# Seven block products for the last eight tiles of the odd batches, and where the weight blocks are stored

## Chip, cores and metric

The kernel runs on one core of one Trainium2 chip. The metric is the device time of one execution in microseconds; before the change it is 752.98 us, the median of 3 runs (750.64 to 752.99). The profile is one execution with a span of 752.0 us.

The engines have short names: PE is TensorE (matmuls, with PEld for its weight loads), DVE is VectorE, ACT is ScalarE, POOL is GpSimd, SP is SyncE. SPq is the queue of transfers (DMA) that SP issues, one after the other in the program's order.

## What is computed

```python
# x (8, 8, 512, 64), state (8, 8, 32, 64): batch, head, token, width
a = softmax(scale * x @ state^T);    xread = a @ state
a2 = softmax(scale * state @ x^T);   sread = a2 @ x
t = concat([xread, sread], axis=2)          # 544 rows for each batch
t = t.transpose(0, 2, 1, 3).reshape(4352, 512)
h = t @ w_in                                # w_in (512, 2048)
g = h * cos(h)                              # the gate
out = g @ w_out                             # w_out (2048, 512)
```

All matmuls are in float32. The weights come as 64-bit floats and are converted on the chip in the first part of the run.

## The kernel before

**Tiles and steps.** The program is one list of tiles. A tile is a slice of 128 of the 2048 columns of h, for the 512 tokens of one batch: 16 tiles f for each of 8 batches b, 128 in all; 16 further tiles at the end serve the state rows. Each step of the outer loop (line 1281) works on one tile, and 32 steps (two batches, a *pair*) make a period. A batch's first eight tiles and its last eight are two phases: phases 0 and 1 are the even batch's, 2 and 3 the odd batch's.

**First layer.** The attention matrix aT (256 rows of softmax weights by 512 tokens) is multiplied with the product of state and w_in (`sw`). In batches 0 and 1 and in phase 3 of the later odd batches this is done plainly: `hidden` (line 485) issues two matmuls of 512 columns for each tile. Elsewhere two tiles that are neighbours share a scheme of seven products of blocks with half the size in each direction, in place of the eight that the blocks of a 2 x 2 product need: `seven_part` (line 529) issues seven matmuls of 256 columns in four parts, two parts in the even step and two in the odd one. It wants more from other engines: `sw_sums` (line 518) makes four sums of 128 x 128 on POOL, three steps ahead; ACT copies two half banks after part 0 (lines 544, 545), before part 1 may add to them; DVE makes two sums in PSUM (`seven_sum`, line 547), one behind part 1 and one behind part 2. `seven` (line 501) says which tiles do this.

**Gate.** ACT rounds h (`gate`, line 561), DVE takes the difference (`gate2`, 564), ACT takes the sine (`gate3`, 567), DVE multiplies (`gate4`, 581, the gate product) and writes g to SBUF. `gate4` frees the PSUM bank into which the first layer of a later tile goes.

**Second layer.** The product of g and w_out is done for a pair of batches with seven products at the outer level ("p1" to "p7"), each of which again has seven block products. g is stored in `quads`, groups of four tiles; `quads_free` lists those that are free. The *outer sums* of quads (`outer_sum`, line 1097, at line 706) are differences of whole quads before a product; their steps are in a table (line 1086). Each block product is a stage (`stage`, line 746) with four matmuls of 256 columns (line 759) against a block of weights that was fetched from DRAM into a ring of four buffers (`fetch_block`, line 693). When a stage has been issued, the fetch for the third stage after it is issued too, and waits until its buffer is free.

**Weight blocks.** w_out gives four matrices a11, a12, a21, a22. Seven matrices (these or sums of them) are each kept in DRAM as eight blocks in `blocks_kept`: numbers 0, 1, 7 and 3 are raw quarters of the matrix, 4, 5, 6 and 2 are sums, made by POOL in `inner_weights` (line 664) and stored by `send` (line 676). Five of the seven are made in steps 7 to 26. Two are late: a22 (number 2) is overwritten in step 18, so it is stored whole in `kept` in step 17 (`move`, line 1106), and read back a quarter at a time in steps 41 to 44 by `late_weights` (line 1113), which then makes its sums in step 45 and stores all eight blocks in steps 46 to 51; a12 (number 1) stays in SBUF, and its eight blocks are stored in steps 52 to 56.

**Order.** Nothing is scheduled by a tool: every engine works in the order in which the program issues. In the first period `first_pair` (line 1186) sets it: `go(n)` issues the attention work that is planned for the step, then come `gate3` and `gate4`. After the tile's work the loop issues what `weights_at` and then `outer_at` hold for the step (lines 1305 to 1308), and at the step's end the loads of x (`load_now`). All transfers but a few share SPq, so a store that waits there holds back the fetches behind it.

Of the kernel before, what the change touches and what calls it, by code (L numbers as in the profile page):

```python
# [10 lines left out]
F32 = mybir.dt.float32  # L11
I32 = mybir.dt.int32
U32 = mybir.dt.uint32
ALU = mybir.AluOpType
# [8 lines left out]
def kernel(  # L23
# [8 lines left out]
    nc = tc.nc  # L32

    B, H, S, D = x.shape
    Ns = state.shape[2]
    Dm, Dff = moe_w_in.shape
    P = 128
# [33 lines left out]
    QT, NQUAD = 4, 12  # L71
# [4 lines left out]
    def quad(n):  # L76
        return g_all[:, QT * n:QT * n + QT]

    def matrix(n):
        return quad(n).rearrange("p t (u d) -> p (t u) d", d=HD)  # L80

    a11, a12, a21, a22 = [matrix(n) for n in range(5, 9)]
# [4 lines left out]
            for i in range(NB)]  # L87
    spare = ctx.enter_context(tc.tile_pool(name="spare", bufs=1,
                                           space=bass.MemoryType.DRAM))
    blocks_kept = spare.tile([7, 8, P, QT * P], F32)  # L90
    kept = spare.tile([QT, P, S], F32)

    xT = consts.tile([P, NK, S], F32)
    x_b = consts.tile([P, NC, H, D], F32)
# [404 lines left out]
    LO, HI = slice(0, HS), slice(HS, S)  # L499

    def seven(t):
        return t.pair is not None and t.b > 1 and t.phase < 3

    def halves(b, n):
        aT, aS = aT_of[b], aS_all[:, b % 2]
# [102 lines left out]
    later, stores_due, totals_due, now = [], [], [], [0]  # L608
# [50 lines left out]
    def quarters(m):  # L659

        m = m.rearrange("p (k i) (m d) -> p m k i d", k=2, m=2)
        return m[:, 0, 0], m[:, 0, 1], m[:, 1, 0], m[:, 1, 1]

    def inner_weights(which, m, temps, pieces=range(4), send_at=None):

        m11, m12, m21, m22 = quarters(m)
        t1, t2, t3, t4 = [temps[:, n].rearrange("p (i d) -> p i d", d=P)
                          for n in range(4)]
        for i in pieces:
            o, x1, x2, op = ((t1, m21, m22, ALU.add),  # L670
                             (t2, t1, m11, ALU.subtract),
                             (t3, m11, m21, ALU.subtract),
                             (t4, m12, t2, ALU.subtract))[i]
            nc.gpsimd.tensor_tensor(o, x1, x2, op=op)

        def send(i):
            block = (m11, m12, m22, m21, t1, t2, t3, t4)[i]
            nc.sync.dma_start(
                out=blocks_kept[which, (0, 1, 3, 7, 4, 5, 6, 2)[i]].rearrange(
                    "p (i d) -> p i d", d=P),  # L680
                in_=block)

        if send_at is None:
            for i in range(4 if 3 in pieces else 0):
                send(i)
                stores_due.append(lambda i=i: send(4 + i))
        else:
            for i, step in enumerate(send_at):
                weights_at[step].append(lambda i=i: send(i))
# [363 lines left out]
    for i, t in enumerate(all_tiles):  # L1053
        t.mate = all_tiles[i ^ 1]
    pairs = [all_tiles[2 * NF * n].pair for n in range(B // 2)]
    stage_at, sums_at, outer_at, weights_at = [defaultdict(list)
                                               for _ in range(4)]
    PERIOD, STAGES = 2 * NF, len(ORDER)
    ROWS = {"p1": 0, "p2": 1, "p5": 0, "p3": 3, "p6": 0, "p7": 2, "p4": 1}

# [22 lines left out]
    dve, pool = nc.vector, nc.gpsimd  # L1083
    for n in range(B // 2):
        end = n == B // 2 - 1
        for r, engine, o, x1, x2, half in (
                ((20, 25) if n == 0 else (25, 26), dve, 0, 2, 0, 0),
                ((27 - (not n), 28), dve, 0, 2, 0, 1), ((31, 31), pool, 2, 3, 2, 0), ((33, 33), dve, 0, 3, 0, 0),
                ((34, 34 + (not end)), dve, 0, 3, 0, 1),
                ((35, 36), dve, 2, 3, 2, 1),  # L1090
                ((38 - end,) * 2, pool, 1, 1, 0, 0),
                ((39 - end,) * 2, pool, 1, 1, 0, 1)):
            for i in range(2):
                outer_at[PERIOD * n + r[i]].append(
                    (engine, n, o, x1, x2, half, i))

    def outer_sum(engine, n, o, x1, x2, half, i):
        o, x1, x2 = [quad(quads_of[n, r][half])[:, 2 * i:2 * i + 2]
                     for r in (o, x1, x2)]
        sub(engine, o, x1, x2)  # L1100
# [2 lines left out]
        o_, x1_, x2_ = [quad(q)[:, 2 * i:2 * i + 2] for q in (o, x1, x2)]  # L1103
        nc.vector.tensor_tensor(o_, x1_, x2_, op=op)

    def move(to_dram, q, i):
        sb = quad(q)[:, i]
        o, x = (kept[i], sb) if to_dram else (sb, kept[i])
        nc.sync.dma_start(out=o, in_=x)

    late_quads = []

    def late_weights(step):
        if step == 41:
            late_quads.append(quads_free.pop(0))
        if step < 45:
            move(False, late_quads[0], step - 41)
        if step == 45:
            late_quads.append(quads_free.pop(0))
            inner_weights(2, matrix(late_quads[0]), quad(late_quads[1]),  # L1120
                          send_at=(46, 46, 47, 47, 49, 49, 50, 51))
        elif step == 52:
            quads_free.append(late_quads[0])
            inner_weights(1, a12, quad(late_quads[1]),
                          send_at=(52, 52, 53, 53, 54, 54, 55, 56))
        elif step == 57:
            quads_free.extend([A12, late_quads[1]])

    A11, A12, A21, A22, SQ = 5, 6, 7, 8, 11
    temps = [quad(TEMPS), aS_all.rearrange("p n i s -> p (n i s)").rearrange(  # L1130
        "p (t s) -> p t s", s=S)]
    for i in range(QT):
        weights_at[7 + i].append(lambda i=i: inner_weights(
            0, a11, temps[0], (i,), () if i < 3 else (15,) * 4 + (16,) * 4))
        weights_at[17].append(lambda i=i: move(True, A22, i))
    for steps, o, x1, x2, op in (
            ((18, 19), A21, A11, A21, ALU.subtract),
            ((22, 23), SQ, A12, A22, ALU.subtract)):
        for i in range(2):
            weights_at[steps[i]].append(  # L1140
                lambda o=o, x1=x1, x2=x2, op=op, i=i: weight_sum(
                    o, x1, x2, op, i))
# [4 lines left out]
            nc.gpsimd.tensor_tensor(o_, x1_, x2_, op=op)  # L1147

    for at_, what in (
            (15, lambda: quads_free.append(10)),  # L1150
            (16, lambda: pool_sum(SQ, A21, A22, ALU.add)),
            (17, lambda: quads_free.append(9)),
            (17, lambda: inner_weights(3, matrix(SQ), temps[1])),
            (18, lambda: pool_sum(A22, SQ, A11, ALU.subtract)),
            (20, lambda: inner_weights(5, matrix(A21), temps[0])),
            (22, lambda: inner_weights(4, matrix(A22), temps[1])),
            (23, lambda: quads_free.append(A11)),
            (24, lambda: inner_weights(6, matrix(SQ), temps[0])),
            (25, lambda: quads_free.append(A21)),
            (27, lambda: quads_free.append(A22)),  # L1160
            (27, lambda: quads_free.append(TEMPS)),
            (28, lambda: quads_free.append(SQ))):
        weights_at[at_].append(what)
    for step in (41, 42, 43, 44, 45, 52, 57):
        weights_at[step].append(lambda step=step: late_weights(step))

    n_stages = 0
# [14 lines left out]
    def go(n):  # L1182
        for p in todo[n]:
            part(*p)

    def first_pair(step, t):
        last, conv = conv_at.get(step - 1, -1), conv_at.get(step, -1)
        if step == 4:
            warm(1, acc[0])
        if step != 1:  # L1190
            hidden(t)
        if step == 0:
            hidden(all_tiles[1])
            warm(3, acc[0])
            gate(t)
            gate2(t)
            convert(3, "bcdf")
            convert(4, "1")
            go(0)
        else:  # L1200
            go(0)
            if step == 5:
                states(1, side_banks[0])
            gate(t)
            gate2(t)
            if step == 3:
                warm(4, acc[0])
                part(0, "products", 1, SIDE)
            go(1)
            go(3)  # L1210
            if step == 1:
                convert(4, "bcdf")
            elif last >= 0 and step < 5:
                convert(last, "bcdf")
            if conv >= 0 and not todo[1]:
                convert(conv, "1")
        gate3(t)
        go(5)
        if step == 3:
            part(0, "products_kept", 1, SIDE)  # L1220
        gate4(t)
        if step == 6:
            states_kept(1, side_banks[0])
        if last >= 0 and 4 < step < 11:
            convert(last, "bcdf")
        if conv >= 0 and todo[1] and step > 0:
            convert(conv, "1")
        go(2)
        if conv >= 0:
            convert(conv, "2")  # L1230
        if step > 10 and conv >= 0 and not todo[1]:
            convert(conv, "bcdf")
        go(4)
        if step > 10 and conv >= 0 and todo[1]:
            convert(conv, "bcdf")
# [126 lines left out]
```

## Time and profile before

| what | value |
|---|---|
| time, median of 3 | 752.98 us |
| PE busy, of the span | 719.7 us, 96% |
| POOL, DVE, ACT busy | 69%, 65%, 44% |
| DMA traffic | 113.42 MB, mean 151 GB/s |
| block fetches (line 697) | 202, of 256 KB, 2.8 us from issue to landing |
| block stores (line 678) from g | 48, of 256 KB, 3.5 us to landing |
| `kept`: stores, loads | 4 and 4, of 256 KB, 3.7 and 3.2 us to landing |
| plain first layer (line 491), 512 columns | 224 records |
| seven-product first layer (line 541), 256 columns | 504 records |

In lines of the timeline the columns are: start and duration in us, engine, line of the kernel, operation, output and inputs, count, and in brackets how long the engine stood idle before it and who ended that. A line of a group has the count, busy time and mean duration, then the idle time. A line of waits has who waited for whom: total, number, longest. A line of a stretch has its bounds, its length, the busy time (and count) of PE, PEld, DVE, ACT and POOL, the granted clock of PE, the share of DMA and GB/s. A time in the profile is counted from the span's start.

The first gate products of batches 2, 4 and 6 start at 178.6, 342.0 and 500.2 us, that of the state tiles at 652.8 us.

### The profile page before, as it was taken

What the parts mean: (1) busy time and instruction counts of PE and PEld (TensorE: products, weight loads), DVE (VectorE), ACT (ScalarE), POOL (GpSimd) and SP (SyncE); (2) the same over time, 40 slices, a digit from 0 to 9 for tenths busy, and PEclk for the clock granted to TensorE, in tenths of its full rate; (3) what the DMA queues carried; (4) which work ended last, traced back from release to release, by engine and by line L of the source; (5) the groups of instructions that cost most, each with busy time, mean ns of one, the idle gap of its engine ahead of it and who ended that gap; (6) DMA issues with size and microseconds to landing.
All of it is one profiled execution on the core that took longest, in us unless ns stands there. A gap on an engine that the chain in (4) does not pass through costs nothing.

```text
span 752.0 us, 10489 instructions
## 1 busy us (share of the span) xinstructions
PE 719.7 (96%) x3552; PEld 507.6 (67%) x3552; DVE 489.9 (65%) x683; ACT 330.7 (44%) x538; POOL 517.4 (69%) x480
## 2 busy tenths in 40 slices
PE   8999888799999899999999999999999999999998
PEld 3443333367768676677778776777688767888886
DVE  4769789776965547668766566859756446364550
ACT  3777872644373435344544454343734332211110
POOL 2355569768998883397998753689989534799600
PEclk9999999999999999999999999999999999999999
DMA  9495499957236975584236835762225455445661
GB/s 250 160 253 204 129 246 297 285 108 169 73 105 141 218 203 171 115 175 119 85 82 139 183 87 103 152 166 82 74 70 120 119 184 138 116 151 187 177 156 40
DMA packets 211509, 113.42 MB, mean 151 GB/s; under 512 B 158400, under 2 KB 173248, under 8 KB 211456
## 3 DMA queue, kind: packets, MB, share of 16 engines
q1 hardware_dynamic: 210368, 112.23, 57.6%
q8 instruction: 28, 0.46, 0.3%
q10 hardware_dynamic: 960, 0.39, 0.2%
q14 instruction: 25, 0.20, 0.1%
q0 software_dynamic: 128, 0.13, 0.1%
HBM read 88.08 MB, written 24.64 MB: 150 GB/s over the span
## 4 chain that ended last, share of the span: by engine, by line
PE 66%; POOL 16%; DVE 8%; ACT 4%; DMA 3%; issue 3%; SPq 0%; DVEq 0%; POOLq 0%; ACTq 0%
PE o L759 33%; PE h L491 13%; POOL g_all L706 12%; PE h L541 9%; PE at L329 3%; PE at L860 2%; POOL swS_all L524 2%; PE at L426 2%; DVE q_all L564 1%; DMA x_b<-in_x_dram 1%; POOL sw L524 1%; ACT q_all L567 1%; PE o L635 1%; PE o L935 1%; DMA g_all<-blocks_kept 1%
## 5 line engine op out<-in xcount | busy, mean ns | idle before, releaser
L706 POOL TENSOR_TENSOR g_all<-g_all 128x512 f32<-128x512 f32 x256 | 335.7, 1343 | 115.7 <-PE o L759 62.3
L759 PE MATMUL o<-g_all 128*128 128x256 f32 x1456 | 344.9, 382 | 5.4 <-DMA g_all<-blocks_kept 3.1
L759 PEld LDWEIGHTS o<-g_all 128*128 128x128 f32 x1456 | 273.7, 190 | 65.6 <-issue 16.1
L491 PE MATMUL h<-aT,sw 128*128 128x512 f32 x224 | 108.3, 607 | 11.7 <-DVE g_all L581 11.1
L564 DVE TENSOR_TENSOR q_all<-q_all,h 128x1024 f32<-128x1024 int32 (+1 forms) x88 | 85.4, 971 | 51.2 <-ACT q_all L561 51.0
L581 DVE TENSOR_TENSOR g_all<-h,q_all 128x1024 f32<-128x1024 f32 (+1 forms) x88 | 85.7, 974 | 37.2 <-ACT q_all L567 37.1
L567 ACT ACTIVATE q_all<-q_all,halfpi 128x1024 f32<-128x1024 f32 (+1 forms) x88 | 84.1, 956 | 55.1 <-DVE q_all L564 54.9
L561 ACT ACTIVATE q_all<-h 128x1024 int32<-128x1024 f32 (+1 forms) x88 | 73.1, 830 | 69.7 <-DVE g_all L581 32.4
L491 PEld LDWEIGHTS h<-aT,sw 128*128 128x128 f32 x224 | 41.1, 191 | 57.7 <-issue 31.4
L550 DVE TENSOR_TENSOR h<-h,sums_all 128x256 f32<-128x256 f32 x72 | 30.9, 429 | 63.2 <-PE h L541 48.5
L706 DVE TENSOR_TENSOR g_all<-g_all 128x1024 f32<-128x1024 f32 x40 | 55.2, 1396 | 0.1
L541 PE MATMUL h<-aS_all,swS_all 128*128 128x256 f32 x144 | 45.7, 399 | 2.6 <-ACT sums_all L545 1.8
L541 PE MATMUL h<-aT,sw 128*128 128x256 f32 x144 | 45.2, 396 | 3.0 <-DVE g_all L581 2.5
L764 ACT COPY o<-o 128x256 f32<-128x256 f32 x26 | 9.3, 357 | 86.8 <-PE o L759 86.8
L258 POOL TENSOR_TENSOR w_in<-w_in,aS_all 128x1024 int32<-128x1024 int32 (+1 forms) x10 | 19.3, 1928 | 37.6 <-DVE w_in L253 18.1
L541 PE MATMUL h<-aS_all,sw 128*128 128x256 f32 x144 | 43.6, 384 | 0.0
L770 ACT COPY o<-sums_all 128x256 f32<-128x256 f32 x26 | 9.8, 378 | 74.2 <-PE o L759 74.2
L604 DVE SCALAR_TENSOR_TENSOR held<-o,held 128x512 f32<-128x512 f32 x40 | 27.1, 680 | 21.3 <-PE o L759 20.8
L462 ACT COPY sw<-at 128x512 f32<-128x512 f32 x50 | 26.8, 588 | 31.2 <-PE at L329 31.2
L541 PEld LDWEIGHTS h<-aS_all,swS_all 128*128 128x128 f32 x144 | 25.7, 191 | 21.7 <-issue 7.0
L541 PEld LDWEIGHTS h<-aT,sw 128*128 128x128 f32 x144 | 26.2, 192 | 12.7 <-DVE g_all L581 9.4
L258 POOL TENSOR_TENSOR g_all<-g_all,aS_all 128x1024 int32<-128x1024 int32 x8 | 19.0, 2370 | 22.4 <-DVE g_all L253 10.4
(115 smaller groups left out, 883.4 us busy)
## 6 DMA issues: line engine op xcount, KB each, us to landing
g_all<-blocks_kept SPq DMA_DIRECT2D x202, 256.0 KB, 2.8
blocks_kept<-g_all SPq DMA_DIRECT2D x48, 256.0 KB, 3.5
g_all<-in_moe_w_out_dram SPq DMA_DIRECT2D x8, 1024.0 KB, 5.0
out_dram<-ot SPq DMA_DIRECT2D x128, 64.0 KB, 2.0
g_all<-in_moe_w_in_dram SPq DMA_DIRECT2D x6, 1024.0 KB, 5.4
xT<-in_x_dram SPq DMA_DIRECT2D x96, 64.0 KB, 2.9
x_b<-in_x_dram SPq DMA_DIRECT2D x24, 256.0 KB, 4.7
x_b<-in_x_dram SPq DMA_DIRECT2D x16, 128.0 KB, 4.3
```

The source lines that it names most:

```text
L258: nc.gpsimd.tensor_tensor(bits, bits, e, op=ALU.add)
L462: (copy or nc.scalar.copy)(sw_of[self.b, nt][:, j, c0:c1], to[j][:, c0:c1])
L491: nc.tensor.matmul(out=t.hp, lhsT=t.lhs(i), rhs=t.rhs(i), start=(i == 0), stop=(i == t.kn - 1))
L541: nc.tensor.matmul(out=out_, lhsT=w, rhs=r, start=start, stop=True, skip_group_check=True)
L550: nc.vector.tensor_tensor(o, h2[:, LO], sums_all[:, 0], op=ALU.add)
L561: nc.scalar.activation(t.q.bitcast(I32), t.hp, func=ACTF.Copy, bias=0.25)
L564: nc.vector.tensor_tensor(t.q, t.q.bitcast(I32), t.hp, op=ALU.subtract)
L567: nc.scalar.activation(t.q, t.q, func=ACTF.Sin, bias=halfpi, scale=-TWO_PI)
L581: nc.vector.tensor_tensor(g, t.hp, t.q, op=ALU.mult)
L604: nc.vector.scalar_tensor_tensor(out=out.t[:, ch], in0=bank, scalar=TWO_PI, in1=b.t[:, ch], op0=ALU.mult, op1=ALU.add)
L706: engine.tensor_tensor(o[:, i:i + n], x1[:, i:i + n], x2[:, i:i + n], op=ALU.subtract)
L759: nc.tensor.matmul(out=o, lhsT=ring[(self.first + k) % NB][:, i], rhs=g[:, i], start=(start and i == 0), stop=(i == QT - 1), skip_group_ch ...
```

## The change

Three things are changed together.

1. `seven` holds for phase 3 as well, so the last eight tiles of batches 3, 5 and 7 do their first layer by seven block products. Twelve pairs of tiles change.
2. `kept` is gone. The raw quarters of a22 and a12 go straight to their places in `blocks_kept` in steps 17 and 19. a22 is read back from these, with all four loads in step 41. The late steps then have only the sums to store: four blocks in steps 49 to 51 and four in 54 to 56.
3. In the first period an outer sum leaves step 20, and the second half of a sum of weights (line 1104, the seventh matrix) leaves step 23. The outer sums of steps 25 and 26 are issued ahead of these steps' `gate3` and `gate4`; the weight sum goes to step 25, and POOL's sums for that matrix go from step 24 to 25.

```diff
     blocks_kept = spare.tile([7, 8, P, QT * P], F32)
-    kept = spare.tile([QT, P, S], F32)
...
     def seven(t):
-        return t.pair is not None and t.b > 1 and t.phase < 3
+        return t.pair is not None and t.b > 1
...
+    def send_raw(which, m, back=False):
+        for i, block in zip((0, 1, 7, 3), quarters(m)):
+            o, x = blocks_of(which, i), block
+            nc.sync.dma_start(out=x if back else o, in_=o if back else x)
...
         if send_at is None:
-            for i in range(4 if 3 in pieces else 0):
-                send(i)
-                stores_due.append(lambda i=i: send(4 + i))
+            send_raw(which, m)
+            stores_due.extend([lambda i=i: send(i) for i in range(4)])
...
-                ((20, 25) if n == 0 else (25, 26), dve, 0, 2, 0, 0),
+                ((25, 26), dve, 0, 2, 0, 0),
...
-                outer_at[PERIOD * n + r[i]].append(
+                at_ = mid_at if n == 0 and r[i] < 27 and r[0] == 25 else outer_at
+                at_[PERIOD * n + r[i]].append(
                     (engine, n, o, x1, x2, half, i))
...
         if step == 41:
             late_quads.append(quads_free.pop(0))
-        if step < 45:
-            move(False, late_quads[0], step - 41)
-        if step == 45:
+            send_raw(2, matrix(late_quads[0]), back=True)
+        elif step == 45:
             late_quads.append(quads_free.pop(0))
             inner_weights(2, matrix(late_quads[0]), quad(late_quads[1]),
-                          send_at=(46, 46, 47, 47, 49, 49, 50, 51))
+                          send_at=(49, 49, 50, 51))
         elif step == 52:
             quads_free.append(late_quads[0])
             inner_weights(1, a12, quad(late_quads[1]),
-                          send_at=(52, 52, 53, 53, 54, 54, 55, 56))
+                          send_at=(54, 54, 55, 56))
...
-            0, a11, temps[0], (i,), () if i < 3 else (15,) * 4 + (16,) * 4))
-        weights_at[17].append(lambda i=i: move(True, A22, i))
+            0, a11, temps[0], (i,), () if i < 3 else (16,) * 4))
...
-            ((22, 23), SQ, A12, A22, ALU.subtract)):
+            ((22, 25), SQ, A12, A22, ALU.subtract)):
...
+            (15, lambda: send_raw(0, a11)),
+            (17, lambda: send_raw(2, a22)),
+            (19, lambda: send_raw(1, a12)),
...
-            (24, lambda: inner_weights(6, matrix(SQ), temps[0])),
+            (25, lambda: inner_weights(6, matrix(SQ), temps[0])),
...
             go(1)
             go(3)
+            for what in mid_at[step]:
+                outer_sum(*what)
```

## The prediction

> **What bounds the kernel now.** I read the page first: busy shares, then the chain that ended last.
>
> ```profile
> PE 719.7 (96%) x3552; PEld 507.6 (67%) x3552; DVE 489.9 (65%) x683; ACT 330.7 (44%) x538; POOL 517.4 (69%) x480
> PE 66%; POOL 16%; DVE 8%; ACT 4%; DMA 3%; issue 3%; SPq 0%; DVEq 0%; POOLq 0%; ACTq 0%
> ```
>
> TensorE (PE) sets the pace, so two things count: how much time its instructions take, and where it stands still. A busy PE is not a PE at its peak, so I take the pace from start times in the timeline, at the border of an odd batch's last eight tiles and the next batch:
>
> ```profile
> 446.62 1.88 PE L491 MATMUL h<-aT,sw 128*128 128x512 f32 x4
> 448.34 1.89 PE L759 MATMUL o<-g_all 128*128 128x256 f32 x8
> 450.06 1.88 PE L491 MATMUL h<-aT,sw 128*128 128x512 f32 x4
> 482.09 0.59 PE L541 MATMUL h<-aS_all,swS_all 128*128 128x256 f32 x2
> 482.52 1.89 PE L759 MATMUL o<-g_all 128*128 128x256 f32 x8
> ```
>
> Four records of 512 columns take 450.06 - 448.34 = 1.72 us like the eight of 256 before them: 429 ns and 215 ns a record. Every f32 matmul leaves two records (line 541 has 504 = 36 pairs x 7 x 2). So a plain matmul of 512 columns costs 858 ns, one of 256 columns 430.
>
> Next the waits, the timeline of the DMA-issuing queue (SPq), and equal stretches of two periods. Batch 3's first tiles (240 to 283 us) and batch 5's (403.2 to 441.5) do the same work:
>
> ```profile
> PE o L759 <- DMA g_all<-blocks_kept: 3.1, 1, 3.1
> ```
> ```profile
> 252.65 0.45 SPq L697 DMA_DIRECT2D g_all<-blocks_kept  x1
> 253.15 1.20 SPq L678 DMA_DIRECT2D blocks_kept<-g_all  x2
> 254.39 4.22 SPq L132 DMA_DIRECT2D x_b<-in_x_dram  x4
> 258.70 2.04 SPq L697 DMA_DIRECT2D g_all<-blocks_kept  x3
> ...
> 263.17 2.58 PE L759 MATMUL o<-g_all 128*128 128x256 f32 x8 [3.09 <-DMA g_all<-blocks_kept]
> ```
> ```profile
> 413.07 0.45 SPq L697 DMA_DIRECT2D g_all<-blocks_kept  x1
> 413.57 3.62 SPq L132 DMA_DIRECT2D x_b<-in_x_dram  x4
> 417.29 2.53 SPq L697 DMA_DIRECT2D g_all<-blocks_kept  x3
> ```
> ```profile
> 240.00:283.00 43.00, 39.91 (x207) 30.78 (x205) 24.27 (x34) 16.09 (x28) 37.55 (x38) 0.96 0.87 205
> 403.20:441.50 38.30, 38.30 (x209) 30.00 (x208) 24.69 (x35) 16.09 (x28) 28.17 (x32) 1.00 0.72 157
> ```
>
> Gate products (line 581) at 239.73 and 281.91 match those at 403.12 and 440.07: 42.18 against 36.95 us, so 5.2 us are lost once. In batch 3 two pairs of raw-block stores (steps 46, 47) stand in SPq ahead of the fetch of the next weights; the fetch goes out at 258.70, while PE, 163.3 us ahead of its twin, would have had it at 417.29 - 163.3 = 254.0. It lands at 263.16, PE waits 3.1 us, and afterwards its records stand some 425 ns apart until 267.9 (granted clock 0.96).
>
> Last, the first period, where VectorE (DVE) is the slower one:
>
> ```profile
> 121.42 1.20 DVE L706 TENSOR_TENSOR g_all<-g_all 128x1024 f32<-128x1024 f32 x1
> 136.08 1.18 DVE L1104 TENSOR_TENSOR g_all<-g_all 128x1024 f32<-128x1024 f32 x1
> 140.26 0.65 DVE L581 TENSOR_TENSOR g_all<-h,q_all 128x512 f32<-128x512 f32 x1
> 140.97 3.24 PE L491 MATMUL h<-aT,sw 128*128 128x512 f32 x4 [2.14 <-DVE g_all L581]
> ```
>
> From 111.5 us to this gate product DVE has three gaps, 3.3 us in all, for which PE waits 2.1 us; both sums are links of the chain.
>
> [...] half pace after the 3.1 us wait, and for some records after the 2.1 us one. [...] the sum of line 1104 takes 1.18 us beside an idle POOL, 2.29 at 112.13 beside a busy one. [...] the median store lands in 3.5 us to the block store and in 3.7 us to the kept matrix, so storing the latter as raw blocks costs nothing more.
>
> **The change, part by part.**
>
> *A, fewer late stores.* Blocks 0, 1, 7, 3 of both late matrices go out at steps 17 and 19; steps 46, 47, 52 and 53 have no store left. The queue of batch 3 up to the critical fetch is then that of batch 5, whose fetch did not hold PE. Gain 5.2 us: 3.1 of wait, the rest half clock. Low end 3.3, if the fetch is still 1 us late and some half clock stays.
>
> *B, seven products instead of four.* Per pair of tiles PE gives up 4 x 858 = 3432 ns and gets 7 x 430 = 3010; I use 408 ns saved (records of 429 and 216). Twelve pairs (four in each of batches 3, 5, 7): 4.9 us. Added beside it per pair: POOL four sums (0.62 + 0.53 + 0.48 + 0.46 = 2.1 us), ACT two copies (0.75), DVE two sums (0.86). POOL hides its 8.4 us in a batch: in the last eight tiles of batch 5 it stood idle for 8.4, 12.7 and 6.8 us at a time. DVE is about 75% busy there. The new waits: PE's second part waits for the ACT copies, and behind attention's exponentials these are late. Where seven products meet them already, this was
>
> ```profile
> 375.75 0.37 ACT L545 COPY sums_all<-h 128x256 f32<-128x256 f32 x1
> 376.26 0.67 PE L541 MATMUL h<-aS_all,swS_all 128*128 128x256 f32 x2 [0.49 <-ACT sums_all L545]
> ```
>
> I count 0.6 us for that (559 + 76 ns of excess between starts), twice, since batch 7 has no attention behind it, and 0.5 us of small waits in all: B = 4.9 - 1.7 = 3.2. Ends: 4.9 with no wait; 0 if each of the three stretches loses 1.6 us, about what the worst stretch of eight tiles with seven products (342.0 to 382.4 us, PE standing still for 2.4 us by the starts of its records) loses beyond the plain one of 440.1 to 480.1 (0.9).
>
> *C, sums in front of gate products.* The first sum leaves step 20 (1.13 us of chain), the other step 23 (1.11). After the first everything moves 1.1 us ahead; after the second ACT's sine, ending at 139.87, becomes the limit for the gate product of 140.26, so only 0.3 more: 1.4 us. Three sums now run at steps 25 and 26. Two lie in the 0.79 us that DVE waits there for the sine, and overhang by about 0.6; PE has 2 us of lead over those gate products, so this costs nothing. A PE wait a little shorter may also spare the half clock (1.3 us); not counted. POOL's sums for the seventh matrix now wait for the sum of step 25 and end near 150 us instead of 143.4; SPq, in order, holds back behind their stores twelve x loads and three fetches. Fetch four then goes out near 155 us and lands near 158; PE wants it at 160.1 - 1.4 = 158.7. The two after it are as tight. I take 0.2 us, ends 0 and 1.
>
> *D, read back at once.* Four loads of 0.43 us at step 41 instead of one a step. The next fetch (219.19) waited for PE anyway. The four stores more at step 19 (3.1 us of SPq) fall where SPq waits for POOL's sums. Together 0.1 us, up to 1.
>
> Sum: 5.2 + 3.2 + 1.4 - 0.2 - 0.1 = 9.5; 752.98 - 9.5 = 743.5 us. PE holds the chain from 141 us on, and the stretch led by POOL (503 to 542) starts from PE's work, so all of it reaches the end.
>
> **Rivals.**
>
> *A new late fetch* (step 26 to 30 or step 41), once long enough to halve the clock again, as costly as the old one: 743.5 + 5.2 = 748.7. For it: the margins in C. Against it: the loads of step 41 fall into a wait of SPq.
>
> *The seven products give nothing* (B = 0): 743.5 + 3.2 = 746.7. For it: DVE and ACT have attention's work there. Against it: batch 5's first tiles do seven products with 0.9 us of standstill, as much as plain ones.
>
> *Slower*: each of the twelve new pairs stalls as the worst old one (382.4 to 385 us: 160 + 104 + 588 + 104 + 436 + 104 ns = 1.5 us): 752.98 - 11.2 + 18.0 = 759.8, where 11.2 is A, C and D with the full 4.9. For it: it happens once a period. Against it: POOL is late there, and in the new place it is idle.
>
> **How the numbers follow.** Forecast 0.69, new late fetch 0.13, nothing from the products 0.13, slower 0.05. 743.5 is the likeliest. Low end: B at 4.9 and the half clock spared, 743.5 - 1.7 - 1.3 = 740.5. High end: the late fetch, 748.7. Faster 0.93, same 0.02, slower 0.05.
>
> **What would show it.** A: no PE wait on a block fetch at 260 us, and the stretch that took 42.18 us near 37. B: 168 more records at line 541's place and 96 fewer of 512 columns; each odd batch's last eight tiles shorter by 0.9 to 1.6 us. C: the gate product of 140.26 near 138.9. Wrong if PE waits for a fetch between 153 and 161 us, if the copies after the exponentials hold PE for more than a microsecond, or if the clock falls below 1.0 anywhere after 145 us.

## The result, and the profile after

The changed kernel takes 744.36 us (median of 743.85 to 744.74); the kernel before, timed on the same chip, 752.99 us. The ratio is 0.9891, interval 0.9869 to 0.9913: 8.2 us less by this ratio, with 6.6 and 9.9 us as ends (the two medians alone are 8.6 us apart). The forecast was 743.5 us, 9.5 us less.

The page of the changed kernel, busy shares and then the chain that ended last, its share by engine:

```profile
PE 711.9 (96%) x3624; PEld 518.4 (70%) x3624; DVE 498.2 (67%) x707; ACT 338.7 (46%) x562; POOL 539.4 (73%) x528
PE 59%; POOL 22%; DVE 6%; ACT 4%; DMA 4%; issue 3%; SPq 2%; DVEq 0%; POOLq 0%; ACTq 0%
```

PE has 7.8 us less to do with 72 records more, POOL 22 us more. PE still leads, but POOL has risen from 16% to 22% of the chain. The groups of costliest instructions show what part B exchanges: line 490 (line 491 before) has 128 records of 512 columns instead of 224, line 540 has 672 of 256 instead of 504.

Now the place of the big wait. The timeline of the DMA-issuing queue and of TensorE in batch 3, at the fetch that came late before:

```profile
246.81 0.46 SPq L700 DMA_DIRECT2D g_all<-blocks_kept  x1
247.31 4.42 SPq L131 DMA_DIRECT2D x_b<-in_x_dram  x4
251.82 2.08 SPq L700 DMA_DIRECT2D g_all<-blocks_kept  x3
```
```profile
256.84 0.59 PE L540 MATMUL h<-aS_all,swS_all 128*128 128x256 f32 x2
257.27 1.89 PE L762 MATMUL o<-g_all 128*128 128x256 f32 x8
```

No store stands between the fetches any more, the fetch goes out at 251.82 instead of 258.70 us (2.6 us of this because the whole stretch starts earlier), and PE goes from line 540 to line 762 at its ordinary pace (0.43 us for two records). The two stretches that the prediction compared, each from one gate product to another (length, then busy time of each engine, granted clock, DMA share, GB/s):

```profile
237.10:274.22 37.12, 37.12 (x203) 29.07 (x202) 23.44 (x33) 16.10 (x28) 35.56 (x40) 1.00 0.79 188
394.85:431.80 36.95, 36.95 (x203) 29.01 (x202) 23.34 (x34) 16.11 (x28) 28.72 (x35) 1.00 0.72 161
```

The stretch of 42.18 us is 37.12, and the twins now agree to 0.2 us.

To see where every microsecond went, I set the start of each gate product (line 580; 581 before) against the same one of the kernel before, and took the change of this difference from step to step. The same is done for the experiments, some of which come further below; "last eight" are the tiles that B changes. Negative is time won, in us:

| stretch (steps) | changed | A alone | B alone | C alone | raw later | raw half | border on GpSimd | the same without C |
|---|---|---|---|---|---|---|---|---|
| start to 16 | -0.92 | -1.01 | -0.86 | -0.74 | -0.39 | -0.68 | +0.84 | -1.17 |
| 16 to 24 | -2.40 | +0.01 | 0.00 | -2.42 | +0.09 | +0.15 | -1.40 | +0.11 |
| 24 to 31 | +0.67 | -0.87 | -0.86 | +0.68 | -0.87 | -0.85 | +0.67 | -0.87 |
| 48 to 52 | -5.05 | -4.68 | -0.07 | -0.56 | -5.05 | -3.66 | -5.05 | -5.05 |
| 52 to 64 (batch 3, last eight) | -0.62 | 0.00 | -0.62 | 0.00 | 0.00 | 0.00 | -1.64 | -1.65 |
| 80 to 96 (batch 5) | -0.61 | +0.38 | -0.61 | 0.00 | 0.00 | 0.00 | -1.64 | -1.65 |
| 116 to 128 (batch 7, last eight) | -1.53 | 0.00 | -1.52 | 0.00 | 0.00 | 0.00 | -1.53 | -1.53 |

The first row is not the change: the very first gate product is already 1.02 us earlier, and kernels with the same code in that stretch lie between -1.17 and +0.84. A good part of it is, by the author's estimate, a spell of half clock at 8.43 us in the trace of before (granted clock 0.50 until 11.84 us); the four traces that have one near 8 us are those with the latest first gate product (29.1 to 29.3 us, the other nine 28.2 to 28.9). The third row holds a second trap. Steps 24 to 31 are the same code in the kernel before, A alone, B alone and the two raw variants, and all four of these are 0.85 to 0.87 us faster than the kernel before. The windows of 140 to 145 us tell why, first of the kernel before, then of A alone:

```profile
140.00:145.00 5.00, 4.04 (x12) 1.78 (x14) 4.21 (x6) 2.70 (x5) 4.62 (x3) 0.66 1.01 296
```
```profile
140.00:145.00 5.00, 4.65 (x24) 2.17 (x24) 4.21 (x5) 2.24 (x4) 3.84 (x4) 1.00 1.01 275
```

The profiled execution of before had a spell of half clock there (0.66) which others of the same code don't have. A comparison of two single traces credits C with 1.74 us between steps 16 and 31; 0.87 of it belongs to this spell.

### The profile page after: what moved, and what is told of

Read it like the earlier page. It is cut to its first block, busy times and chain, and to the rows that moved or that the text cites. A ratio compares the mean times of both kernels' runs of the same rounds, so it can differ in the third digit from the quotient of the medians.

```text
span 742.1 us, 10759 instructions
## 1 busy us (share of the span) xinstructions
PE 711.9 (96%) x3624; PEld 518.4 (70%) x3624; DVE 498.2 (67%) x707; ACT 338.7 (46%) x562; POOL 539.4 (73%) x528
## 4 chain that ended last, share of the span: by engine, by line
PE 59%; POOL 22%; DVE 6%; ACT 4%; DMA 4%; issue 3%; SPq 2%; DVEq 0%; POOLq 0%; ACTq 0%
PE o L762 30%; POOL g_all L709 15%; PE h L540 13%; PE h L490 5%; PE at L328 3%; POOL swS_all L523 2%; PE at L863 2%; PE at L425 2%; POOL sw L523 1%; DVE g_all L709 1%; POOL g_all L1144 1%; DMA x_b<-in_x_dram 1%; SPq L669 1%; PE o L938 1%; PE o L863 1%
## 5 line engine op out<-in xcount | busy, mean ns | idle before, releaser
L549 DVE TENSOR_TENSOR h<-h,sums_all 128x256 f32<-128x256 f32 x96 | 41.2, 429 | 76.1 <-PE h L540 58.2
L490 PE MATMUL h<-aT,sw 128*128 128x512 f32 x128 | 61.6, 605 | 10.9 <-DVE g_all L580 10.3
L540 PE MATMUL h<-aS_all,swS_all 128*128 128x256 f32 x192 | 60.3, 396 | 3.2 <-ACT sums_all L544 1.8
L540 PE MATMUL h<-aT,sw 128*128 128x256 f32 x192 | 59.6, 392 | 3.8 <-DVE g_all L580 3.4
L540 PE MATMUL h<-aS_all,sw 128*128 128x256 f32 x192 | 58.1, 384 | 0.2
L709 DVE TENSOR_TENSOR g_all<-g_all 128x1024 f32<-128x1024 f32 x40 | 57.2, 1447 | 0.1
L540 PEld LDWEIGHTS h<-aS_all,swS_all 128*128 128x128 f32 x192 | 33.8, 189 | 27.9 <-issue 11.3
L490 PEld LDWEIGHTS h<-aT,sw 128*128 128x128 f32 x128 | 22.8, 189 | 43.4 <-DVE g_all L580 19.3
L540 PEld LDWEIGHTS h<-aT,sw 128*128 128x128 f32 x192 | 34.5, 189 | 16.3 <-DVE g_all L580 12.2
L523 POOL TENSOR_TENSOR swS_all<-sw 128x128 f32<-128x128 f32 x48 | 22.8, 475 | 29.1 <-ACT sw L461 29.1
L540 PEld LDWEIGHTS h<-aS_all,sw 128*128 128x128 f32 x192 | 35.6, 190 | 8.4 <-DVE h L549 2.8
```

The lines of the kernel that those rows point to most:

```text
L490: nc.tensor.matmul(out=t.hp, lhsT=t.lhs(i), rhs=t.rhs(i), start=(i == 0), stop=(i == t.kn - 1))
L540: nc.tensor.matmul(out=out_, lhsT=w, rhs=r, start=start, stop=True, skip_group_check=True)
L549: nc.vector.tensor_tensor(o, h2[:, LO], sums_all[:, 0], op=ALU.add)
L709: engine.tensor_tensor(o[:, i:i + n], x1[:, i:i + n], x2[:, i:i + n], op=ALU.subtract)
```

## The experiments

**A alone.** The changed kernel with B and C taken back:

```
-        return t.pair is not None and t.b > 1
+        return t.pair is not None and t.b > 1 and t.phase < 3
...
-                ((25, 26), dve, 0, 2, 0, 0),
+                ((20, 25) if n == 0 else (25, 26), dve, 0, 2, 0, 0),
...
-            ((22, 25), SQ, A12, A22, ALU.subtract)):
+            ((22, 23), SQ, A12, A22, ALU.subtract)):
...
-            (25, lambda: inner_weights(6, matrix(SQ), temps[0])),
+            (24, lambda: inner_weights(6, matrix(SQ), temps[0])),
```

> Part A with D alone: the late matrices' raw blocks are stored in steps 17 and 19, read back in step 41, and only the four sums of each are stored late; first layer and order of sums as before. Theory (the stores stood in the queue in front of the fetch): 5 us less than before, near 748; no wait of TensorE for a block fetch near 260 us, gate products of steps 48 and 56 near 37.8 us apart instead of 42.9, full clock there. Rival 1 (part of the gain in that stretch came only because B or C moved the work against the transfers): the wait stays in part, 749 to 752. Rival 2 (the read back of four blocks at once, or the four stores more at step 19, cost something that B or C hid): a new wait near 150 or 220 us, 749 or more.

Measured: 749.19 us, ratio 0.9951 (0.9937 to 0.9964), 3.7 us less (2.7 to 4.7). In the trace the stretch is 4.68 us shorter, and a wait of 0.26 us for a block fetch, and 0.10 behind it, are left at 258.4 us. The theory holds for the place and the wait, though the executions gained 3.7 us where it had 5; of rival 1 no more than these 0.37 us is true. They are absent in the changed kernel, and also where nothing but these stores is moved (below), so the fetch is in time by a hair only: the loads of x ahead of it held the queue for 4.56 us here, 4.42 and 4.13 us there. Nothing new at 150 or 220 us: rival 2 falls. The 0.38 us that batch 5 took more is the same stop again one period later, before the block product at 416.95 us; it lies in batch 5's first eight tiles, which the change of B does not touch.

**B alone.** The kernel before with the first of these lines only, in the other direction.

> Part B alone: seven block products also in the last eight tiles of batches 3, 5 and 7, nothing else changed. Theory (what the changed kernel showed stretch by stretch adds up): 0.6 + 0.6 + 1.5 us in the three stretches, 2.75 less than before, near 750.2, and near 1 us of standstill at each border of batch 3 to 4 and 5 to 6 for a gate product. Rival 1 (that standstill came from B together with A or C): no standstill there, 1.5 us in each stretch, near 748.4. Rival 2 (VectorE's and GpSimd's added work lengthens the half-clock stretch of batch 3): batch 3 gains nothing, 751 or more.

Measured: 749.87 us, ratio 0.9963 (0.9948 to 0.9978), 2.8 us less (1.7 to 3.9), and stretch by stretch the same 0.6, 0.6 and 1.5 us as in the changed kernel. The stops at the border are there as well (0.24 + 0.10 and 0.59 + 0.10 us at 320 us): B makes them by itself, rivals 1 and 2 fall.

**C alone.** The kernel before with the sums moved as in the changed kernel.

> Part C alone: outer sums of the first period in steps 25 and 26, in front of the gate products, the second half of the weight sum in step 25, the seventh matrix's sums after it. Theory: gate product of step 24 about 2.4 us earlier against that of step 16, 0.7 to 1.1 us of it given back by step 31, net about 1.7 us, near 751.3. Rival 1 (the give-back is due to the four stores more of step 19 and not to the moved sums): net 2.4 us, near 750.6. Rival 2 (GpSimd's late sums delay the fetches behind their stores): TensorE waits for a block fetch between 150 and 165 us, 753 or more.

Measured: 751.54 us, ratio 0.9986 (0.9973 to 0.9999), 1.1 us less (0.1 to 2.0). The trace repeats the changed kernel's: 2.42 us won by step 24, 0.68 given back against a kernel before that stood at half clock itself. Rival 1 falls, since the four stores more of step 19 are not in this kernel; so does rival 2.

**Order or bytes?** The kernel before with its raw stores in other steps:

```
-                          send_at=(46, 46, 47, 47, 49, 49, 50, 51))
+                          send_at=(49, 49, 50, 50, 49, 50, 51, 51))
```

> The kernel before with the same eight stores of the first late matrix, the same bytes and the same run length, but the four raw ones issued in steps 49 and 50 instead of 46 and 47, behind the fetch that came late. Theory (order in the queue): most of A's gain, 4 to 5 us, near 748.5, no wait near 260 us. Rival (the bytes of these stores, or the transfers' own time, hold the fetch back): the wait only moves by two or three steps, the time stays within 1.5 us of before.

Measured: 747.78 us, ratio 0.9937 (0.9925 to 0.9950), 4.7 us less (3.8 to 5.6); the stretch is 5.05 us shorter, as in the changed kernel. The same bytes cost nothing behind the fetch. The rival falls: A's gain is the order in the queue. Moving these four stores alone gained no less than the whole of A with its read back (3.7 us; the two intervals overlap).

**Half the dose.** The same with (46, 46, 50, 50, 49, 49, 50, 51): two of the four stores stay in front.

> The kernel before with half of the dose: two raw stores stay in step 46, in front of the late fetch, the two of step 47 go to step 50. Theory (each store ahead of the fetch delays it by its own time in the queue, and the slow records after the wait come from the length of the wait): TensorE waits 1 to 2 us for the fetch instead of 3.1, and with the shorter wait the 2 us of half clock after it are gone too; gates of steps 48 and 52 near 20.4 to 21 us apart instead of 24.5; time 748 to 749.5. Rival (the slow records have nothing to do with the wait's length): the wait shrinks but some 2 us of slow records stay, gates near 22.5 us apart, time near 750.

Measured: 750.38 us, ratio 0.9966 (0.9954 to 0.9979), 2.6 us less (1.6 to 3.5). Timeline and windows around the fetch:

```profile
259.77 1.99 PE L759 MATMUL o<-g_all 128*128 128x256 f32 x8 [1.11 <-DMA g_all<-blocks_kept]
```
```profile
258.00:266.00 8.00, 6.89 (x44) 4.89 (x42) 5.24 (x9) 3.05 (x5) 5.66 (x9) 1.00 1.11 309
```

A wait of 1.11 us instead of 3.09, and the clock stays at 1.00 where it was halved before. Gate products 48 and 52 are 20.81 us apart (24.48 before), inside the theory's 20.4 to 21; the executions, 750.4, came out slower than its 748 to 749.5. In the traces half of the stores costs 1.4 us and all of them 5.05: the second half costs more than twice the first. Half clock followed the wait of 3.09 us (granted clock 0.50 from 264.43 to 267.84 us), not the one of 1.11. The executions do not show this: there half of the stores costs 4.7 - 2.6 = 2.1 us and the other half 2.6, about the same, each known to within 1 us or so. The profiled execution is the fastest of the seven (748.7 us), and the mean clock of three others is 0.995 against its 0.997, so they had more half clock than this trace; where is not on record.

The wait was followed by half clock in all three traces where it lasted 2.5 us or more (before, B alone, C alone: granted clock 0.89 from 255 to 270 us in each, against 1.00 in the half dose). But four of the thirteen executions of C alone have a mean clock of 1.000, hence less than 0.8 us of half clock; they took 749.2 to 749.4 us, the other nine 750.8 to 752.5. So half clock after this wait does not come every time; the last section shows what it goes with in the traces.

**Where B loses in batches 3 and 5.** The changed kernel at the border of batches 5 and 6, DVE and PE:

```profile
467.59 1.22 DVE L709 TENSOR_TENSOR g_all<-g_all 128x1024 f32<-128x1024 f32 x1
468.72 0.42 DVE L509 TENSOR_TENSOR aS_all<-aT 128x256 f32<-128x256 f32 x1
469.17 1.38 DVE L509 TENSOR_TENSOR aS_all<-aT,aS_all 128x256 f32<-128x256 f32 x1
470.47 0.68 DVE L603 SCALAR_TENSOR_TENSOR held<-o,held 128x512 f32<-128x512 f32 x1
471.07 0.42 DVE L549 TENSOR_TENSOR h<-h,sums_all 128x256 f32<-128x256 f32 x1
471.40 1.21 DVE L580 TENSOR_TENSOR g_all<-h,q_all 128x1024 f32<-128x1024 f32 x1
...
472.67 0.70 PE L540 MATMUL h<-aT,sw 128*128 128x256 f32 x2 [0.42 <-DVE g_all L580]
```

DVE runs without a gap from 467.25 us on: an outer sum, two differences for the next batch, an eviction, the seven products' sum, and only then the gate product that PE waits for. POOL is idle until 468.95. So one outer sum goes there:

```
+                border = 0 < n < B // 2 - 1 and r[i] == 28
                 at_[PERIOD * n + r[i]].append(
-                    (engine, n, o, x1, x2, half, i))
+                    (pool if border else engine, n, o, x1, x2, half, i))
```

> The changed kernel with one outer sum in step 28 of the second and third periods moved from VectorE to GpSimd, which stands idle there. Theory (B gains only 0.6 us in batches 3 and 5 because at the batches' border VectorE, full with outer sum, differences, evictions and now the seven products' sums, is 1 us late with the gate product): the two waits at 314 and 472 us vanish, each of these stretches becomes 0.9 to 1.0 us shorter, 2.0 us in all, time near 742.4. Rival 1 (VectorE's queue is held by something else, such as the sum of the block products, which waits for TensorE): the waits stay, time 744.4. Rival 2 (GpSimd beside VectorE slows both, and the sums for the next batch's seven products come late): a new wait for those sums near 315 and 473 us, time 744.4 or more.

Measured: 743.28 us, ratio 0.9870 (0.9855 to 0.9886). Both stretches win 1.64 us against before, 1.03 more than in the changed kernel, and the waits are gone:

```profile
466.68 2.51 POOL L709 TENSOR_TENSOR g_all<-g_all 128x512 f32<-128x512 f32 x2 [2.44 <-DVE g_all L709]
...
471.79 1.22 DVE L580 TENSOR_TENSOR g_all<-h,q_all 128x1024 f32<-128x1024 f32 x1
...
472.98 0.59 PE L540 MATMUL h<-aS_all,sw 128*128 128x256 f32 x2
473.41 0.59 PE L540 MATMUL h<-aT,sw 128*128 128x256 f32 x2
```

The gate product begins 1.62 us ahead of the records of line 540 that need it, which follow without a stop; in the changed kernel it was 1.27, with PE waiting. The theory holds to 0.05 us; 1.64 us is what the prediction's 408 ns for each of four pairs gives without any wait (1.63). The executions' gain over the changed kernel is not resolved by these two intervals, but two other pairs that differ in this move alone, below, don't overlap.

**Where C loses.** After step 24 the changed kernel's DVE and PE:

```profile
141.00 1.22 DVE L1108 TENSOR_TENSOR g_all<-g_all 128x1024 f32<-128x1024 f32 x1
...
142.30 6.92 POOL L681 TENSOR_TENSOR g_all<-g_all 128x512 f32<-128x512 f32 x4 [8.01 <-DVE g_all L1108]
142.74 1.92 DVE L709 TENSOR_TENSOR g_all<-g_all 128x1024 f32<-128x1024 f32 x1
...
145.18 1.69 DVE L709 TENSOR_TENSOR g_all<-g_all 128x1024 f32<-128x1024 f32 x1
...
147.38 1.18 DVE L435 TENSOR_TENSOR sr<-at,i 32x128 f32<-32x128 f32 x4
...
148.62 1.09 PE L328 MATMUL at<-w_in,st_all 64*32 64x512 f32 x16 [0.84 <-DVE sr L435]
```

The moved half of the weight sum ends at 142.2 and lets POOL begin the seventh matrix's sums. Beside them the two outer sums take 1.92 and 1.69 us instead of 1.2, line 435, which frees a bank, comes late, and PE waits. At 156 us PE stands still another 0.72 us, because POOL's first sums for batch 2's seven products are late behind this (0.18 in A alone). As a first attempt, the weight sum and the seventh matrix go back to steps 23 and 24, and the outer sums stay:

> The changed kernel with one part of C undone: the second half of the weight sum again in step 23 and the seventh matrix's sums on GpSimd again in step 24; the outer sums stay in front of the gate products. Theory (that move won 0.3 us at the gate product of step 24 and cost more later, because GpSimd's sums then run beside VectorE's outer sums, 1.9 and 1.7 us instead of 1.2, and a bank is freed 0.9 us late, and because the first sums for the seven products of batch 2 come 0.5 us late): 0.3 us later at step 24, no wait of 1.0 us near 148.6 us, under 0.3 us near 156 us; by step 31 0.9 us ahead of the changed kernel, time near 743.5. Rival (the sum on step 24's path costs its full 1.1 us): no net gain, 744.4 to 744.8.

Measured: 745.46 us, ratio 0.9899 (0.9886 to 0.9912). This is slower than the changed kernel and than the rival's 744.4 to 744.8. The theory fell on its first number: in step 23 the sum ran beside POOL and took 2.26 us, the gate product of step 24 came 1.4 us later than in the changed kernel (counted from step 16), not 0.3, PE waited

```profile
139.20 3.78 PE L490 MATMUL h<-aT,sw 128*128 128x512 f32 x4 [3.21 <-DVE g_all L580]
```

for it, and half clock followed (granted clock 0.50 from 140 to 145 us). The waits at 148.6 and 156 us went as foretold, but by step 31 this kernel is 1.85 us behind the changed one. With the border move added:

> Both of these moves in the changed kernel. Theory: they lie in different places of the run, so their gains add, 0.9 + 2.0 us, time near 741.5 and 1.4% less than before. Rival (a stretch after one of them is limited by an engine that does not start earlier): less than the sum, 742.5 or more.

Measured: 742.94 us (742.33 to 743.55), ratio 0.9865 (0.9850 to 0.9880), against 745.46 (744.3 to 745.81) on the same chip without the border move. With the first move lost the sum of 2.9 us is lost too; the border move brought 2.5 us here, 2.0 were expected of it. In a second attempt at C this half is made by POOL in step 23, and the seventh matrix behind it in step 24 (the lines below are the new branch alone):

```
+        if on_pool:
+            for k in (2, 3):
+                nc.gpsimd.tensor_tensor(quad(o)[:, k], quad(x1)[:, k],
+                                        quad(x2)[:, k], op=op)
+            return
```

> The changed kernel with the second half of the weight sum on GpSimd in step 23 (two sums of 512 columns) and the seventh matrix's sums behind it in step 24; VectorE has neither that half in step 23 nor in step 25. Theory (C's gain by step 24 is given back by step 31 because GpSimd's sums of the seventh matrix, waiting for VectorE's half in step 25, run beside VectorE's outer sums and in front of the sums for batch 2's first seven products): GpSimd, idle from 134 to 142 us, ends these sums near 144 instead of 149; the waits of 1.0 us near 148.6 and 0.7 us near 156 us fall below 0.3; from step 24 to 31 the kernel gains 0.8 us against the kernel before's undisturbed pace instead of losing 0.7; 1.0 to 1.5 us less than the changed kernel, near 743.5. Rival 1 (GpSimd beside VectorE from 134 us on delays the gate product of step 24 as much): step 24 later by 0.5 us or more, no gain. Rival 2 (something else limits steps 28 to 31): waits vanish, no gain by step 31.

Measured: 744.14 us (743.58 to 744.96), ratio 0.9885 (0.9868 to 0.9901), no gain that can be told. The waits at 149 and 156 us fell to 0.28 and 0.47 us, but PE stood idle 1.05 us before 142.6 us for a gate product, where it was 0.46 in the changed kernel: all three outer sums of DVE now ran beside POOL and took 1.69, 2.32 and 1.69 us. The gate product of step 24 came 0.24 us later, less than the 0.5 of the first rival. From step 24 to 31 0.35 us is given back instead of 0.67. With the border move:

> The changed kernel with both of these: weight sum's second half on GpSimd, and the outer sum at the batches' borders on GpSimd. Theory: the gains lie apart and add, 1.2 + 2.0 us: near 741.5, 1.5% less than before. Rival (the first period's gain is lost again): as the border move alone, near 743.3.

Measured: 742.50 us (741.37 to 742.9), ratio 0.9860 (0.9845 to 0.9875), 1.64 us less than without that move, ranges apart. It is the lowest of all, though not told apart from the border move alone, and lies between the theory's 741.5 and the rival's 743.3.

**What is C worth?** The border move with C taken back:

> The changed kernel with the border move and without C (first period's sums as in the kernel before). What is C worth? Theory (of what C wins by step 24 all but 0 to 1 us is given back by step 31; the rest of what the traces of before and after differ by there is a spell of half clock in the profiled run of before): 0.5 to 1 us slower than the border move with C, near 744, and by the gate products of steps 16 and 31 no more than 0.9 us between them. Rival (C is worth the 1.4 to 1.7 us that the comparison of the two traces shows): 1.4 us or more, near 745.

Measured: 743.57 us, ratio 0.9876 (0.9859 to 0.9894), against 743.28 with C: 0.3 us, not resolved. From step 16 to the end of the tiles the two traces differ by 0.06 us. The rival's 1.4 us is not seen, though the executions alone don't exclude it: the two intervals leave room for some 2 us either way, and C alone gained 0.1 to 2.0. By the traces C is worth -0.1 us, as in this pair, or 0.9; which of the two goes with which engine's sum took longer in step 18 (last section).

## Why the prediction was right

**A, right in cause, and in size for the traces.** Forecast 5.2 us: 3.1 of wait and the rest half clock. The stretch was 5.05 us shorter in the trace of the changed kernel, 4.68 where A was alone. The executions of A alone gained less, 3.7 us with 4.7 as upper end: the forecast took its 2 us of half clock from one profile as if they came every time, and they do not (C alone and the half dose, above). That order in the queue is the cause is shown by the raw stores put behind the fetch. After the stop of 2.1 us, too, half pace did not come every time: none followed in A alone or B alone (granted clock 1.00 from 140 to 145 us), where this stop is as long to 0.01 us (last section).

One reading of the lines names the wrong span: from 448.34 to 450.06 us run the eight records of 256 columns; the four of 512 run from 446.62 to 448.34. Both are 1.72 us, so the two paces stand.

**B, right in sum, wrong in where it loses.** Forecast 4.9 - 1.7 = 3.2 us; measured 0.62 + 0.61 + 1.53, 2.75 us. The step that failed is the wait of 0.6 us for ACT's copies behind the exponentials. It did not occur:

```profile
443.30 0.37 ACT L544 COPY sums_all<-h 128x256 f32<-128x256 f32 x1
...
444.06 1.09 PE L328 MATMUL at<-w_in,st_all 64*32 64x512 f32 x16
...
445.08 0.70 PE L540 MATMUL h<-aS_all,swS_all 128*128 128x256 f32 x2
```

The copies end at 443.67, and PE, with a block product and a projection in between, wants the second part at 445.08. In their place stood DVE's full queue at the border, 1.03 us twice (0.24, 0.10, 0.59 and 0.10 us). The prediction had read "about 75% busy" as room; the share is a mean, and the border is the place where it is 100%. The summed wait, 4.9 - 2.75 = 2.15 us, is near the 1.7 assumed, so the sum held by luck.

**C, right up to step 24, then wrong.** Forecast 1.4 us by the gate product of step 24. The border move's trace has exactly 1.40, the changed kernel 2.40; the 1.0 more goes with which of two engines' sums took longer in step 18, told below. Then "the overhang of 0.6 us costs nothing, PE has 2 us of lead" failed. Next to POOL the sums took 0.7 and 0.5 us more than 1.2, and from step 24 to 31 C gives back 1.54 us against kernels of the same code without it (+0.67 to -0.87). The prediction had put only 0.2 us there, for late fetches, and no fetch was late. Net -0.1 or 0.9 us instead of 1.2, with one outcome or the other; a half-clock spell more or less comes on top.

**D and the rivals.** Reading back at once cost nothing (0.02 us from step 31 to 48; 0.1 forecast). No PE wait for a block fetch appears from 153 to 161 us, and the clock record of the changed kernel shows no half clock before 740.95 us, when PE has no work left, so the first rival fell. B gave something, so the second did too. The worst new pairs lost 1.0 us and only once a batch, so the third fell.

**The sum.** The terms measured, 5.05 + 2.75 and 0 to 0.9 for C, give 7.8 to 8.7 us; the three parts timed alone 3.7 + 2.8 + 1.1 = 7.6; the whole 8.2. The forecast was too high by 1.3 us, about what C failed to bring and B lost.

## What to carry to other kernels

A store that nobody waits for can cost more than the wait it causes, if it stands in an in-order queue in front of a load (here 5.05 us in the trace, with a wait of 3.09); look at what is queued between two fetches, and compare with a twin stretch where it is not. Put a price on a moved instruction at the place where it lands: read the busy gaps of that engine there, and whether another engine runs at that moment (a DVE sum took 1.18 us beside an idle POOL and up to 2.32 beside a busy one), not its average share. And before a part of a change is credited with a microsecond, look at the same stretch in several traces of unchanged code.

## What the runs showed of the hardware

In step 18 a DVE sum of 1024 columns and a POOL sum of 512 start 0.03 to 0.06 us apart, POOL first, in all thirteen traces. The kernel before, then the changed one:

```profile
112.08 1.26 POOL L674 TENSOR_TENSOR aS_all<-g_all 128x512 f32<-128x512 f32 x1
112.13 2.29 DVE L1104 TENSOR_TENSOR g_all<-g_all 128x1024 f32<-128x1024 f32 x1
```
```profile
111.16 2.37 POOL L681 TENSOR_TENSOR aS_all<-g_all 128x512 f32<-128x512 f32 x1
111.21 1.18 DVE L1108 TENSOR_TENSOR g_all<-g_all 128x1024 f32<-128x1024 f32 x1
```

One of the two takes its shorter time, 1.18 us on DVE or 1.26 to 1.27 on POOL, and the other some 1.1 us more: POOL took 2.35 to 2.37 us in eight traces, DVE 2.29 or 2.30 in five, with the same code. The recorded starts order the outcomes: in the five traces where POOL's is 0.052 to 0.057 us ahead, DVE's sum is the longer one; in the eight where it is 0.028 to 0.047 us ahead, POOL's is. So a few hundredths of a microsecond go with the outcome; what shifts them from run to run, and why one sum is longer, was not shown. Where DVE's is the longer one, the gate product of step 19 comes 1.1 us later. Without C this is mostly gone by step 24; with C it stays, and is 1.0 of the 2.40 us that C seemed to win.

By the clock records of the traces a spell of half clock (0.50) lasts 3.41 us (one lasts twice that, and the end of the run cuts the last), and in one trace all start whole multiples of 3.413 us apart: in the kernel before at 8.43, 141.55 and 264.43 us, 39 and 36 times that apart. The pace of the matmuls agrees with these records: after the third start they stand 425 ns apart, until 267.9 us, where 215 is the pace at a clock of 1.00. The three stretches of 3.41 us around the second start, with PE busy for 1.27 us in the one ahead of it:

```profile
138.14:141.55 3.41, 1.27 (x4) 0.35 (x3) 3.34 (x5) 2.21 (x3) 3.33 (x4) 1.00 1.01 284
141.55:144.96 3.41, 3.41 (x12) 1.39 (x12) 2.62 (x4) 2.34 (x4) 3.07 (x2) 0.50 1.02 303
144.96:148.37 3.41, 3.41 (x32) 1.94 (x28) 2.62 (x4) 1.32 (x2) 1.27 (x1) 1.00 1.02 313
```

With all thirteen traces cut into stretches of 3.413 us from these starts, and those counted that begin before 738 us, ten have PE idle for 2.14 us or more, and half clock follows each of them in the next stretch (in the kernel before, after 2.14 us from 138.14 and 2.16 from 261.01 us). Sixteen have it idle for 1.75 to 1.87 us, and it follows seven (in the same trace after 1.76 us from 5.02, but not after 1.79 from 131.31 us). It follows none of the rest, but for one stretch that ran at half clock itself (weight sum back, from 138.13 us, 1.07 us idle). So in these traces half clock goes not with the length of a stop but with how much of it falls into one such stretch, and these lie differently against the kernel's start in each trace (counted back, the first begins at 1.60 us in the kernel before and at 0.26 in the changed one). Thus the stop before the gate product of step 24 was followed by half clock in the kernel before but not in A alone, B alone, the half dose and the border move without C, where it is as long to 0.01 us: there no stretch held more than 1.70 us of it. In the kernel before with its raw stores later an even longer stop, 2.5 us, was not followed, with 1.82 us in the fuller stretch. One profile shows one such draw.
